# Diagonal score pieces of a gated attention kernel, cut row block by row block, with their halves on alternating PE halves and three DMA turns each

## The chip, the cores and the metric

The kernel runs on one core of a Trainium2 chip. The metric is the device time of one execution in microseconds (us); lower is better. The median of four executions of the kernel before is 1201.04 us (1200.83 to 1202.45). The engines are called by the profile's short names: PE (TensorE matmul), PEld (its weight loads), DVE (VectorE), ACT (ScalarE), POOL (GpSimd) and SP (the queue that issues most DMAs).

## The reference

```python
batch, seq, d_model = (8, 3008, 256)
d_qk = 64

def _attn_ref(u, v, z):
    scale = 1.0 / S
    scores = scale * np.matmul(z, z.transpose(0, 2, 1))
    attn = np.maximum(scores, 0.0) ** 2
    out = np.matmul(attn, v)
    return (u * out).astype(np.float32)

def _moe_ref(x, w_in, w_out):      # x: 24064 x 256, w_in: 256 x 2048
    h = x @ w_in
    g = h * np.cos(h)
    return (g @ w_out).astype(np.float32)
```

The scores come from z on both sides, so the matrix of scores of a batch is symmetric: the block of rows k and columns j is the transpose of the block of rows j and columns k. The change lives on this.

## The kernel before

**Pieces.** A batch's 3008 x 3008 scores are cut into row blocks k of 128 rows (24, the last of 64) and column groups J of 512 columns (6, the last of 448). Four row blocks make a row group I, and a piece (b, J, I) is the 512 x 512 part of batch b in column group J and row group I, held in one of 18 buffers A as relu(score) squared, in fp16. Only pieces with I >= J are computed, in two groups each, h = 0 (row blocks 4I and 4I+1) and h = 1 (4I+2 and 4I+3). The pieces above the diagonal are made by turning those below with a DMA that transposes blocks of 128 x 128. (For the first three column groups of batch 0 more is computed directly, and nothing on the diagonal is cut.)

**A score group** (`emit_score`, L182 to L224). Two matmuls at L191 write two banks of an accumulator E, one for each of the two row blocks t = 0, 1. The contraction has 64 rows. zT holds z transposed twice, on partitions 0 to 63 and again on 64 to 127, so the two matmuls can take the two halves of the PE array: t = 0 half 0, t = 1 half 1. ACT then takes the relu of both banks to r (L204), and DVE squares r into the piece's buffer (L209, or L212 on the diagonal). Once a piece is whole, it is entered in a list of pieces to be turned.

**Pieces on the diagonal** (I = J, 45 of them are cut). In its group h = 0 only the first 256 columns are computed (`W = 2 * P`), in h = 1 all. What is missing, rows 0 to 255 of columns 256 to 511, is turned from the lower left of the same piece.

**Turns** (`emit_turns`, L226 to L246). In order of the slot that needs them, SP issues one turn of 16 blocks for a piece off the diagonal (L244, into a fresh buffer) and two turns of 2 blocks for one on it (L238): for rr = 2 and 3, the row block rr's first two blocks into column block rr of rows 0 and 1.

**Value matmuls** (`emit_value`, from L257). For slot s = (b, J), `phase_a` contracts the pieces of column group J with v, in two passes over 24 row blocks, again with 64 rows at a time: t = 0 on half 0, t = 1 on half 1, always in this turn, each into a bank of its own. Between these pairs, `phase_a` puts the score groups of later slots (some three slots ahead) at even distances, each followed by `emit_turns` of one more turn. `phase_a` thus consists of half-array matmuls alone.

**Expert layers.** `phase_b` follows each `phase_a`: with the full array, h = x w_in (L403), the cosine on ACT (L411), the product on DVE (L414), and g w_out (L465 or L507). Half-array and full-array work take turns 46 times in a run.

**Order.** The program is written out by hand (`manual_schedule`): each engine runs its instructions in the order in which the code emits them, and waits for others by semaphores. SP's queue holds the turns of scores (L238, L244), of u (L160) and of z (L133), and the stores of the output (L525 to L529, L560). POOL's queue holds the loads of u, v and z (L118 to L146) and the additions on GpSimd. The landing of each of SP's DMAs is told by one of eight semaphores in turn, so an instruction that needs several DMAs waits for several semaphores.

Of the kernel before, what the change touches and what calls it, by code (L numbers as in the profile page):

```python
# [14 lines left out]
def kernel(  # L15
# [16 lines left out]
    P = 128  # L32
    H = P // 2
    CW = 512
# [12 lines left out]
    def width(J):  # L47
        return CW if J < NC - 1 else WL
# [38 lines left out]
    def new_piece(key):  # L87
        pieces[key] = free_pieces.pop(0)
        return piece_bufs[pieces[key]]

    def piece(key):
        return piece_bufs[pieces[key]]
# [10 lines left out]
    def take_e():  # L103
        i = e_order.pop(0)
        e_order.append(i)
        return i
# [75 lines left out]
    def emit_score(on_dve=False, later=None):  # L182
        b, J, I, h = groups[done_groups[0]]
        done_groups[0] += 1
        cut = I == J and not (b == 0 and J < 3)
        W = 2 * P if cut and h == 0 else width(J)
        zT = zTs[b]
        e = E[take_e()]
        for t in range(2):
            k = 4 * I + 2 * h + t  # L190
            nc.tensor.matmul(  # L191
                e[:, t, 0:W],
                zT[t * H:(t + 1) * H, k * P:(k + 1) * P],
                zT[t * H:(t + 1) * H, J * CW:J * CW + W],
                start=True,
                stop=True,
            )
        key = (b, J, I)
        a = new_piece(key) if h == 0 else piece(key)
        r = rpool.tile([P, 2, CW], FP16, name="r")  # L200
        if on_dve:
            nc.vector.tensor_scalar(r[:, :, 0:W], e[:, :, 0:W], 0.0, None, ALU.max)
        else:
            nc.scalar.activation(r[:, :, 0:W], e[:, :, 0:W], AF.Relu)  # L204
        def square():
            if I > J:
                a4 = a.rearrange("p (k t j) -> p t k j", k=4, j=P)[:, 2 * h:2 * h + 2, :, :]
                r4 = r.rearrange("p t (k j) -> p t k j", j=P)
                nc.vector.tensor_tensor(a4, r4, r4, ALU.mult)  # L209
            else:  # L210
                a4 = a.rearrange("p (k w) -> p k w", w=CW)[:, 2 * h:2 * h + 2, 0:W]
                nc.vector.tensor_tensor(a4, r[:, :, 0:W], r[:, :, 0:W], ALU.mult)  # L212

        if later is None:
            square()
        else:
            later.append(square)
        if h == 0:
            return
        if cut or (I > J and (b, J, I) not in direct):  # L220
            turns.append(((b, I), key))
            turns.sort(key=lambda t: t[0])
            turn_slots[key] = pieces[key]
            pending[pieces[key]] = "held"  # L224

    def emit_turns(due, more=0):  # L226
        while turns and (turns[0][0] <= due or more > 0):
            if turns[0][0] > due:
                more -= 1
            (b, c), key = turns.pop(0)  # L230
            b, J, I = key
            i = turn_slots[key]
            a = piece_bufs[i]
            if I == J:
                a4 = a.rearrange("p (k w) -> p k w", w=CW)
                for rr in range(2, 4):
                    rows = P if J * 4 + rr < NB - 1 else H
                    nc.sync.dma_start_transpose(  # L238
                        a4[:, 0:2, rr * P:rr * P + rows],
                        a[0:rows, rr * CW:rr * CW + 2 * P],  # L240
                    )
            else:
                d = new_piece((b, I, J))
                nc.sync.dma_start_transpose(d.rearrange("p (n j) -> p n j", j=P), a)  # L244
            if pending.pop(i) == "dropped":
                free_pieces.append(i)  # L246
# [58 lines left out]
    def phase_a(s):  # L305
        b, J = s // NC, s % NC
        emit_turns((b, J))
        n = next_scores(s)
        at = {}
# [7 lines left out]
        for i, (dh, k) in enumerate(steps):  # L317
            if dh == 2:
                emit_value(b, J, k, 0, 0, M[0], False, True)
                emit_value(b, J, k, 1, 1, acc1[1], True, False)  # L320
                gate(s, 0, M[0], M[1])
            else:
                acc = M if dh == 0 else acc1
                last = k == NB - 2
                for t in range(2):
                    emit_value(
                        b, J, k, t, dh, acc[t],
                        k == 0 and not (dh == 1 and t == 1),
                        last and not (dh == 0 and t == 0),
                    )  # L330
                if dh == 1 and (k % 4 == 3 or last):
                    drop_piece((b, J, k // 4))
            for _ in range(at.get(i, 0)):
                emit_score()
                emit_turns(divmod(s + 1, NC), 1)
            if i in mix_at and mixed(s - 2):
                mix_late(s - 2, *mix_at[i])
# [9 lines left out]
    def phase_a_first(s, n, extra={}):  # L347
# [16 lines left out]
        for i, (dh, k) in enumerate(steps):  # L364
            if i in extra:
                extra[i]()
            if dh == 2:
                emit_value(b, J, last, 0, 0, acc[0][0], False, True)
                emit_value(b, J, last, 1, 1, acc[1][1], False, True)
            else:  # L370
                for t in range(2):
                    emit_value(
                        b, J, k, t, dh, acc[dh][t], k == 0, k == last - 1 and t != dh
                    )
            if dh > 0 and (k % 4 == 3):
                drop_piece((b, J, k // 4))
                if s > 0:
                    emit_turns((0, 0), 1)
                    if k < 4:
                        turn_u(s)  # L380
                    elif k < 8:
                        for d in range(2):
                            gate_mul(s - 1, d, late_sums.pop(0))
            for _ in range(at.get(i, 0)):
                emit_score(on_dve=done_groups[0] in on_dve)
# [262 lines left out]
    turn_on_pe(1)  # L648
    copy_turned(1)
    emit_score(later=squares)  # L650
    emit_score(later=squares)
    turn_on_pe(2)
# [46 lines left out]
    for s in range(3, NSLOT + 1):  # L699
        b, J = s // NC, s % NC  # L700
# [52 lines left out]
```

## Time and profile before

| what | value |
|---|---|
| median of four executions | 1201.04 us |
| the profiled execution, its own time | 1201.03 us |
| its span, from the first instruction to the last | 1199.2 us |
| PE clock granted | full throughout |
| L191, 64 x 256 columns, matmuls | 90, busy 12.5 us |
| L191, 64 x 512 columns, matmuls | 578, busy 111.5 us |
| L258, value matmuls | 4512 |
| L204 relu of 128 x 512 (cut groups) | 45, 601 ns each |
| L212 square of 128 x 512 (cut groups) | 45, 418 ns each |
| turns of pieces (L238 and L244) | 90 and 117 |
| share of 16 DMA engines, SP's queue and POOL's | 52.5% and 28.5% |

A row of a group shows the engine, the line, what is written and read, the shape, the count, the time in which at least one of them ran ("busy") and the mean of one. A matmul's duration in such a row includes its latency, and matmuls overlap; what a matmul costs is better read from the distance of starts. In the chain of waits each row is a start in us, the time that the step holds the chain, and what ran.

### The profile page before, as it was taken

The numbers are of one execution on the slowest core, as the hardware profiler recorded it, in microseconds if no ns is written. First come the engines' busy times: TensorE is split into PE (matmuls) and PEld (weight loads), VectorE is DVE, ScalarE is ACT, GpSimd is POOL, SyncE is SP. The second block draws the span as 40 slices with busy tenths as digits, with TensorE's granted clock in tenths as the row PEclk, the third lists the DMA queues.
The fourth block names the chain that finished last, engine by engine and source line by source line (L and its number), as shares of the span: only waits on it lengthen the run. The fifth ranks groups of instructions, "written<-read, shape, count | busy, mean of one in ns | idle before, by whom it ended". The sixth has DMA issues, their size and how long they took to land.

```text
span 1199.2 us, 28321 instructions
## 1 busy us (share of the span) xinstructions
PE 1188.9 (99%) x11695; PEld 703.9 (59%) x11695; DVE 989.5 (83%) x1248; ACT 795.7 (66%) x923; POOL 642.3 (54%) x657
## 2 busy tenths in 40 slices
PE   9999999999999999999999999999999999999998
PEld 4455655665556655665556655665556555666566
DVE  6858888888988887788988889788888888878775
ACT  7957666666766666666766676666766667666444
POOL 3155735567555571665746656166565765525440
PEclk9999999999999999999999999999999999999999
DMA  9998898759996599946999469983798837974301
GB/s 158 179 158 142 133 148 114 122 103 130 133 124 120 105 135 158 130 78 119 140 144 136 79 111 149 164 114 76 114 160 151 117 71 117 165 118 89 62 19 54
DMA packets 467410, 145.13 MB, mean 121 GB/s; under 512 B 391760, under 2 KB 467024, under 8 KB 467280
## 3 DMA queue, kind: packets, MB, share of 16 engines
q1 hardware_dynamic: 368304, 110.11, 52.5%
q0 software_dynamic: 97440, 32.78, 28.5%
q8 instruction: 91, 1.49, 0.5%
q10 hardware_dynamic: 1536, 0.43, 0.2%
q14 instruction: 39, 0.32, 0.1%
HBM read 66.32 MB, written 24.64 MB: 76 GB/s over the span
## 4 chain that ended last, share of the span: by engine, by line
PE 96%; ACT 1%; DVE 1%; issue 1%; DVEq 0%; ACTq 0%
PE E L403 27%; PE M L465 21%; PE M L258 20%; PE E L258 19%; PE E L191 5%; PE M L507 4%; ACT r L204 1%; DVE g L414 0%; PE E L636 0%; DVE A L209 0%; DVE sm L270 0%; DVE A L212 0%; PE E L507 0%; DVE x L286 0%; PE M L660 0%
## 5 line engine op out<-in xcount | busy, mean ns | idle before, releaser
L411 ACT ACTIVATE c<-E 128x1024 f16<-128x1024 f32 (+1 forms) x384 | 385.7, 1006 | 224.1 <-PE E L403 223.2
L414 DVE SCALAR_TENSOR_TENSOR g<-E,c 128x1024 f16<-128x1024 f32 (+1 forms) x384 | 459.0, 1197 | 77.5 <-ACT c L411 77.0
L204 ACT ACTIVATE r<-E 128x512 f16<-128x512 f32 (+1 forms) x342 | 327.8, 966 | 115.1 <-PE E L191 110.1
L258 PEld LDWEIGHTS <-v 64*128 64x128 f16 x4512 | 225.7, 94 | 251.9 <-issue 18.4
L403 PE MATMUL E<-x,w_in 128*128 128x512 f16 (+1 forms) x1408 | 354.5, 375 | 2.7 <-DVE sm L270 2.0
L258 PE MATMUL M<-A,v 64*128 64x512 f16 (+1 forms) x2256 | 283.1, 372 | 0.3 <-DVE sm L270 0.3
L427 POOL TENSOR_TENSOR s<-g 128x512 f16<-128x512 f16 x160 | 187.1, 1169 | 176.1 <-DVE g L414 134.2
L258 PE MATMUL E<-A,v 64*128 64x512 f16 (+1 forms) x2256 | 278.1, 372 | 0.0
L428 POOL TENSOR_TENSOR g<-g 128x512 f16<-128x512 f16 x160 | 198.2, 1238 | 12.6
L403 PEld LDWEIGHTS <-w_in 128*128 128x128 f16 x1536 | 134.6, 98 | 112.4 <-issue 22.7
L209 DVE TENSOR_TENSOR A<-r 128x1024 f16<-128x1024 f16 x240 | 172.5, 730 | 21.6 <-ACT r L204 20.9
L286 POOL TENSOR_TENSOR x<-sm,uT 128x512 f16<-128x512 f32 (+1 forms) x43 | 48.6, 1130 | 244.8 <-DVE sm L270 244.5
L465 PEld LDWEIGHTS <-g 128*128 128x128 f16 x2560 | 156.4, 98 | 36.1
L465 PEld LDWEIGHTS <-s 128*128 128x128 f16 x1920 | 117.3, 98 | 27.0
L191 PE MATMUL E<-zT 64*128 64x512 f16 (+2 forms) x684 | 126.8, 363 | 1.9 <-DVE zT L631 1.1
L433 DVE TENSOR_TENSOR s<-s,g 128x1024 f16<-128x1024 f16 x80 | 90.9, 1136 | 2.1 <-POOL s L427 2.1
L212 DVE TENSOR_TENSOR A<-r 128x512 f16<-128x512 f16 (+1 forms) x102 | 76.9, 755 | 14.8 <-ACT r L204 14.3
L465 PE MATMUL M<-w_mix,s 128*128 128x128 f16 x1280 | 84.6, 219 | 0.0
L465 PE MATMUL M<-w_mix,g 128*128 128x128 f16 x1280 | 84.6, 219 | 0.0
L465 PE MATMUL M<-w_out,g 128*128 128x128 f16 x1280 | 84.6, 219 | 0.0
L191 PEld LDWEIGHTS <-zT 64*128 64x128 f16 x684 | 35.6, 94 | 41.7 <-issue 4.1
L507 PE MATMUL M<-w_out,g 128*128 128x256 f16 x432 | 55.8, 273 | 0.4 <-DVE sm L270 0.4
(55 smaller groups left out, 685.6 us busy)
## 6 DMA issues: line engine op xcount, KB each, us to landing
out_dram<-o SPq DMA_DIRECT2D x87, 256.0 KB, 2.2
v<-in_v_dram POOLq DMA_DIRECT2D x40, 256.0 KB, 8.7
u<-in_u_dram POOLq DMA_DIRECT2D x40, 256.0 KB, 4.8
A<-A SPq DMA_TRANSPOSE x207, 5.4
z<-in_z_dram POOLq DMA_DIRECT2D x14, 192.0 KB, 10.6
z<-in_z_dram POOLq DMA_DIRECT2D x14, 176.0 KB, 5.9
v<-in_v_dram POOLq DMA_DIRECT2D x8, 192.0 KB, 12.3
u<-in_u_dram POOLq DMA_DIRECT2D x8, 192.0 KB, 4.0
```

Of the source, the lines that this page charges most:

```text
L191: nc.tensor.matmul(e[:, t, 0:W], zT[t * H:(t + 1) * H, k * P:(k + 1) * P], zT[t * H:(t + 1) * H, J * CW:J * CW + W], start=True, stop=True,)
L204: nc.scalar.activation(r[:, :, 0:W], e[:, :, 0:W], AF.Relu)
L209: nc.vector.tensor_tensor(a4, r4, r4, ALU.mult)
L258: nc.tensor.matmul(bank[:, 0:width(J)], vs[b, k // 4][t * H:(t + 1) * H, k % 4, dh * P:(dh + 1) * P], value_rhs(b, J, k, t), start=start, ...
L403: nc.tensor.matmul(e[:, f, 0:W], w_in16[:, k, ft * P:(ft + 1) * P], x[:, k, 0:W], start=(k == 0), stop=(k == 1),)
L411: nc.scalar.activation(c[:, :, 0:W], e[:, :, 0:W], AF.Sin, bias=half_pi, scale=inv_s2)
L414: return lambda: nc.vector.scalar_tensor_tensor(gs[m][:, 2 * i:2 * i + 2, 0:W], e[:, :, 0:W], 1.0, c[:, :, 0:W], ALU.mult, ALU.mult)
L427: nc.gpsimd.tensor_tensor(s1[:, f, :], g[:, f, T:], g[:, lower, T:], ALU.add)
L428: nc.gpsimd.tensor_tensor(g[:, f, T:], g[:, f, 0:T], g[:, f, T:], ALU.subtract)
L433: nc.vector.tensor_tensor(s2[:, f, :], s1[:, f, :], g[:, f, 0:T], ALU.subtract)
L465: nc.tensor.matmul(acc[:, k * P:(k + 1) * P], left[:, ft, k * P:(k + 1) * P], right[:, ft, :], start=(ft == 0 and k == 0), stop=(ft == F - ...
L507: nc.tensor.matmul(y_bank(m, k), gs[m][:, ft, k * P:(k + 1) * P], w_out16[:, ft, :], start=(ft == 0 and (k % 2 == 0 or (final and k == 3)) ...
```

## The change

In `emit_score`, each matmul of a cut piece gets its own width, `Wt`: row block 0 has 128 columns, 1 has 256, 2 has 384, and 3 all of them (512, or 448 in the last column group). The half of the array follows t for h = 0, and is the other one for h = 1; this holds for every score group, cut or not. The relu and the square keep the width W of the whole group. In `emit_turns`, a piece on the diagonal has three turns, rr = 1, 2 and 3, of rr blocks each.

```diff
@@ emit_score
         for t in range(2):
             k = 4 * I + 2 * h + t
+            half = t if h == 0 else 1 - t
+            rows = slice(half * H, (half + 1) * H)
+            Wt = min(W, (2 * h + t + 1) * P) if cut else W
             nc.tensor.matmul(
-                e[:, t, 0:W],
-                zT[t * H:(t + 1) * H, k * P:(k + 1) * P],
-                zT[t * H:(t + 1) * H, J * CW:J * CW + W],
+                e[:, t, 0:Wt],
+                zT[rows, k * P:(k + 1) * P],
+                zT[rows, J * CW:J * CW + Wt],
                 start=True,
                 stop=True,
             )
@@ emit_turns
-                for rr in range(2, 4):
+                for rr in range(1, 4):
                     rows = P if J * 4 + rr < NB - 1 else H
                     nc.sync.dma_start_transpose(
-                        a4[:, 0:2, rr * P:rr * P + rows],
-                        a[0:rows, rr * CW:rr * CW + 2 * P],
+                        a4[:, 0:rr, rr * P:rr * P + rows],
+                        a[0:rows, rr * CW:rr * CW + rr * P],
                     )
```

## The prediction

> **What bounds the kernel now.** I read the page first (share of the span by engine, then the chain that ended last), then the chain piece by piece between 300 and 330 us, then the timeline of PE at a change from half arrays to full ones, and last the transfers.
>
> ```profile
> span 1199.2 us, 28321 instructions
> PE 1188.9 (99%) x11695; PEld 703.9 (59%) x11695; DVE 989.5 (83%) x1248; ACT 795.7 (66%) x923; POOL 642.3 (54%) x657
> PE 96%; ACT 1%; DVE 1%; issue 1%; DVEq 0%; ACTq 0%
> ```
>
> TensorE is busy all the time and is 96% of the chain. A busy PE need not be at its peak, so the next view is the chain itself, with the time that each step holds the chain:
>
> ```profile
> 321.10 1.40 PE M L258 x12
> 322.51 0.11 PE E L191 x2
> 322.62 1.08 PE M L258 x10
> 323.69 0.22 PE E L191 x2
> ```
>
> This is a score piece on the diagonal (L191): its upper half is the pair at 322.51, its lower half the pair at 323.69, with ten value matmuls (L258) between. All of these contract 64 rows, so two run at once, one on partitions 0 to 63 (half 0) and one on 64 to 127 (half 1). Ten matmuls of 512 columns take 1.08 us, that is 0.216 us for a pair; a pair of 256 columns takes 0.11 us. So the time goes by the columns, 0.42 ns each, and not by the "270" or "376" ns that a matmul's row shows, which hold its latency too. Placed by their starts in this way, the 11,695 matmuls leave next to no gap from 100 us on, but for one kind:
>
> ```profile
> 305.73 0.38 PE L191 MATMUL E<-zT 64*128 64x512 f16 x2
> 305.95 1.89 PE L258 MATMUL E<-A,v 64*128 64x512 f16 x16
> 307.77 1.04 PE L403 MATMUL E<-xodd,w_in 128*128 128x512 f16 x4
> ```
>
> Eight pairs from 305.95 end at 307.68; the full array starts at 307.77, 0.09 us later. The same 0.09 us stands at nearly every change between half and full arrays. So the end is set by TensorE's columns, and what this change is worth is the columns that really leave the longer half.
>
> **What goes.** 45 diagonal pieces are cut (3 of batch 0, 6 of each of the other seven). Upper half: the first matmul goes from 256 to 128 columns, the second stays at 256. Lower half: the first from 512 to 384, the second stays at 512 (for the 8 pieces of the last column, 448 to 384, and 448 stays). In each pair only one gets shorter. In the upper half the short one is on half 0; in the lower half the program issues the short one first, and on half 1, then the long one on half 0. If both were on half 0, half 1 would be as long as before and nothing could come of it. As it is, half 0 saves 128 columns in the upper pair and half 1 saves 128 in the lower, 54 ns each. To bank them, half 0 must run 54 ns ahead from the upper pair to the lower one. In 39 of the 45 pieces both pairs lie in the same stretch of half-array work; in 6 full-array work comes between, which waits for both halves and loses the lead.
>
> **The size, from both sides.** That a lead can last is seen in the trace: from 197.9 to 209.0 us half 1 starts its matmuls 39 to 55 ns after half 0, through 54 pairs, with neither half closing up. At best, then: 37 pieces x 54 ns + 8 x 27 ns = 2.2 us, less the 6 that lose it (0.3 us) = 1.9 us. At worst nothing: at the lower pair the order is value matmul on half 0, value matmul on half 1, short score on half 1, long score on half 0. Half 0 is free 54 ns before half 1, but the long score stands behind the short one in PE's stream. If PE starts matmuls in program order, the long one waits for the short one's start, and the 54 ns are idle on half 0. From there the long score of 512 columns ends at the very instant at which it ended before; half 1 is done 54 ns earlier, but its next value matmul stands behind that of half 0, and waits likewise. The gain is 0 on every piece. No row decides it: in the profiled program the halves alternate strictly, half 0 first, so no matmul ever stands behind one of the other half that is later.
>
> **Two rules of the Trainium skill pull apart here.** "TensorEngine Tiling (Array Packing)", section "Key Properties", says that tiles work independently and can run matmuls in parallel; taken alone it promises the 1.9 us, and the lasting lag of 39 to 55 ns agrees with it. "TensorE: Matmul & The Clock Gate", section "Part 3: Packing small matmuls", says that matmuls start and end in program order, a strict FIFO in which only weight loads are pulled ahead. By that the sum is 0. The trace agrees as far as it goes (pairs start in step, 3 ns within a pair as a rule), but has no place that could contradict it. The two fit together: independent once started, started in order. I take 0 here.
>
> **The turned order has a price of its own, and more pieces pay it than gain.** The new line for the half looks at h alone, so each of the 171 lower pairs changes order, the 45 cut ones and 126 whole ones. Within a pair the second matmul starts about 3 ns after the first. The first score takes half 1 at +3 ns, the second half 0 at +6, so half 0 resumes some 6.6 ns late: 171 x 6.6 ns = 1.1 us, if matmuls start in order; if not, half 0 never waits and it is 0. Weight loads should be no obstacle: each half's next load starts 2 ns after the matmul before it on that half has started, under it, and in the new order too every load has the length of a matmul to run in. But two matmuls in succession on one half stand nowhere in the trace, so the bounds of a turn are 0 and the 0.09 us of the nearest row, the change of array shape. I take the 6.6 ns, by the rows of pairs, since the shape (64 x 128) stays.
>
> **The engines behind.** ScalarE's relu (L204) and VectorE's square (L212) still take the full width, 256 or the column's, reading leftovers in the corner that the third turn then writes over; 45 relus of 601 ns and 45 squares of 418 ns stay. No gain, no cost.
>
> **The turns.** Per piece two turned transfers of 2 blocks become three of 1, 2 and 3: 45 more issues on the SP queue and 90 more blocks of 128 x 128.
>
> ```profile
> L238 SPq DMA_TRANSPOSE A<-A x90: 1167/1202/2432, 59.3 to 1117.0; - x90
> DMA to landing us min/median/max: 2.3/4.7/9.1
> ```
>
> One issue holds SP 1.2 us whatever its 2 blocks, and an 8-block one of u 1.6, so the sum is 45 x 1.2 = 54 us on a queue whose issues now add up to 675 of 1199 us; 1.2 to 1.6 us later for what is queued behind. What is queued: turns of other pieces (landing 15.8 us or more before the first matmul that reads them), of u (9 us or more after slot 0, mostly 27 to 41), of z (11.8 us or more), and stores of the output (over 10 us before their buffer is written again; the last few, which have less, come after all turns). The diagonal turns themselves land 14 to 42 us before their use, except those of the first cut piece: issued at 59.3 and 60.9 us, the second lands 9.1 us later, 5.1 us before its value matmul at 75.1. The third one, issued at about 62.5, should land near 72: 3 us left. So the queue costs 0 while TensorE covers it. Load of the DMA engines: a block is 128 packets of 256 B of 26 ns over 16 engines, 0.21 us; 90 blocks are 19 us, 1.6% of the span. The tightest transfers are the loads of v at a batch's change (window 280 to 300 us, DMA share 1.39): 3.0 us of slack, of which one piece takes 0.4. Were this cover gone, each late microsecond would be one of the span.
>
> Weight loads that wait for two transfers or more rise from 8 to 46; the first of the two then stands as an instruction of its own on PE, 51 ns in the 7 places at batch starts that have it now, without a gap in the matmuls there, since PE's sequencer is over a microsecond ahead. Bounds 0 and 38 x 51 ns = 1.9 us; I take 0, by those rows.
>
> **Sum.** The profiled execution took 1201.03 us (span 1199.2 and 1.8 around it), the median is 1201.04: 1201.03 - 0 + 1.1 = **1202.1 us**.
>
> **Rivals.**
> - *The halves do slip past each other* (each takes its matmul when it is free): 1201.03 - 1.9 = 1199.1 us. For it: the persistent lag. Against it: order of issue. Chance 0.25. It is 0.16%, so even the full gain lies inside the 0.2% (2.4 us) that a measurement of this kernel can tell from no change.
> - *Turning the order of the halves drains the array*: at the full 0.09 us for each of 171 lower pairs 15.4 us, 1216.4 us. It decides from 14 ns a turn (2.4 us). For it: nothing in the trace has run in this order, and it is paid 171 times against 45 gains. Against it: the shape stays, and weights are loaded under a matmul of the same half already. Chance 0.20.
> - *A transfer comes late*: the third turn at 75 us, or v at the seven changes of batch. It needs more than 3 us of extra delay, then perhaps 0.5 us each, 3.5 us in all: 1204.5 us. Chance 0.05.
>
> **Numbers.** The main case 0.48, the rivals 0.25, 0.20 and 0.05, and 0.02 for something else. Faster by over 0.2% needs more than the slip can give: 0.05, for the slip with luck. Slower by over 0.2%: the drain, late transfers, or the main case with the waits on PE added: 0.27. Within: 0.68. The range takes in the first two cases, the 1.9 us of waits on PE on top of the main one, and turns of up to some 23 ns: 1198.8 to 1205.0 us.
>
> **What would show it.** Right: in the chain the upper pair of a cut piece holds 0.05 us and then half 1 trails by 54 ns; at the lower pair both scores start within 4 ns of each other, the first as late as half 1 is free, and from the upper pair's start to the end of the stretch nothing is shorter than before. The slip is shown if the long score starts before the short one, or the stretch is 54 ns shorter per piece. The drain is shown by a gap of up to 0.09 us at every lower pair, cut or not; late transfers by waits of value matmuls for A or v. I am wrong outright if the time leaves 1198.6 to 1203.4, the bounds of no change.

## The result and the profile after

The changed kernel takes 1199.67 us (median of 41 runs, 1199.30 to 1201.45), the one before 1201.03 us (61 runs). The ratio is 0.999, with a 95% interval of 0.9985 to 0.9994. The profiled execution took 1199.69 us, 1.34 us less than before's, with a span of 1197.9 us. In the kernel before and in most of those below, a part of the executions takes 1.1 to 1.5 us longer, and in the four profiles that fell among them (e6, e7, e9, e10) TensorE's clock is halved for 3.4 us near 90 us (the last section shows it), so a median depends on how many of them it holds. Below, TensorE's part is therefore read from the starts of its matmuls in the trace, after that place.

The page of the changed kernel, the lines that answer to those shown of before:

```profile
span 1197.9 us, 28487 instructions
PE 1187.1 (99%) x11695; PEld 734.6 (61%) x11695; DVE 989.6 (83%) x1248; ACT 795.6 (66%) x923; POOL 642.8 (54%) x657
PE 96%; ACT 1%; DVE 1%; issue 1%; DVEq 0%; ACTq 0%
```

TensorE still sets the end. The chain of the changed kernel, at the piece that was shown of before (start, time that the step holds the chain, what ran):

```profile
320.67 1.40 PE M L261 x12
322.08 0.11 PE E L194 x2
322.19 1.08 PE M L261 x10
323.26 0.16 PE E L194 x2
323.43 0.86 PE M L261 x8
```

The upper pair still holds the chain for 0.11 us, the length of its long matmul, but the lower pair holds it for 0.16 us where it held 0.22. That is 54 ns, the 128 columns. So the columns saved on half 0 in the upper pair and those saved on half 1 in the lower pair were both banked: the halves slipped past each other. The timeline of the changed kernel around another piece shows the slip itself (start, time until the last of the group ends, group):

```profile
102.86 0.27 PE L194 MATMUL E<-zT 64*128 64x128 f16 x2
102.92 1.30 PE L261 MATMUL M<-A,v 64*128 64x512 f16 x10
104.00 0.38 PE L194 MATMUL E<-zT 64*128 64x512 f16 x2
104.21 0.81 PE L261 MATMUL M<-A,v 64*128 64x512 f16 x6
```

The first value matmul starts 0.06 us after the upper pair, when the 128-column one is done. A group carries the shape of its first member by time: the upper pair is headed by the 128-column matmul, the lower one by the one of 512 columns. In the program the 384-column matmul stands first. Each start in the trace:

| start, us | matmul | place in the program |
|---|---|---|
| 103.995 | score, 512 columns, half 0 | second of the lower pair |
| 104.052 | score, 384 columns, half 1 | first of the lower pair |
| 104.211 | value, 512 columns, half 0 | next pair, first |
| 104.214 | value, 512 columns, half 1 | next pair, second |

The halves of the two value matmuls follow from the scores before them: each starts when the score on its half is through (512 columns 216 ns, 384 columns 162 ns). The long score did not wait for the short one that stands ahead of it. Both halves are level again at 104.21, and the stretch from the upper pair to there is 53 ns shorter than before.

Summed over the run: TensorE's last matmul ends 1.84 us earlier than before, in steps of 52 to 55 ns in each stretch of half-array work with one whole cut piece, about 80 in those with one of the last column group beside it, and 2 to 4 ns where a lower pair lies alone. (The first cut piece, in the stretch from 41.9 us on, gained nothing; TensorE waits for other engines there.) From the last matmul to the last instruction, though, it is 4.35 us where it was 3.84. So 1.84 - 0.51 = 1.33 us of the span remain.

### The profile page after: what moved, and what is told of

The parts are those of the page before. It is cut to its first block, busy times and chain, and to the rows that moved or that the text cites. A ratio compares the mean times of both kernels' runs of the same rounds, so it can differ in the third digit from the quotient of the medians.

```text
span 1197.9 us, 28487 instructions
## 1 busy us (share of the span) xinstructions
PE 1187.1 (99%) x11695; PEld 734.6 (61%) x11695; DVE 989.6 (83%) x1248; ACT 795.6 (66%) x923; POOL 642.8 (54%) x657
## 3 DMA queue, kind: packets, MB, share of 16 engines
q1 hardware_dynamic: 380752, 112.93, 54.5%
## 4 chain that ended last, share of the span: by engine, by line
PE 96%; ACT 1%; DVE 1%; issue 1%; DVEq 0%; ACTq 0%
PE E L406 27%; PE M L468 21%; PE M L261 20%; PE E L261 19%; PE E L194 5%; PE M L510 4%; ACT r L207 1%; DVE g L417 0%; PE E L639 0%; DVE A L212 0%; DVE sm L273 0%; DVE A L215 0%; PE E L510 0%; DVE x L289 0%; PE M L663 0%
## 5 line engine op out<-in xcount | busy, mean ns | idle before, releaser
L261 PEld LDWEIGHTS <-v 64*128 64x128 f16 x4512 | 252.6, 94 | 223.2 <-issue 19.6
L194 PE MATMUL E<-zT 64*128 64x512 f16 (+4 forms) x684 | 128.9, 357 | 1.9 <-DVE zT L634 1.1
L194 PEld LDWEIGHTS <-zT 64*128 64x128 f16 x684 | 39.6, 94 | 37.6 <-issue 3.7
```

Of the source, the lines that this page charges most:

```text
L194: nc.tensor.matmul(e[:, t, 0:Wt], zT[rows, k * P:(k + 1) * P], zT[rows, J * CW:J * CW + Wt], start=True, stop=True,)
L261: nc.tensor.matmul(bank[:, 0:width(J)], vs[b, k // 4][t * H:(t + 1) * H, k % 4, dh * P:(dh + 1) * P], value_rhs(b, J, k, t), start=start, ...
```

## Experiments

Starts are compared with those of the kernel before, from the half-array stretch at 101.6 us to the last one; the changed kernel gains 1.76 us there (the other 0.08 us lie earlier). "Tail" is the time from the end of the last matmul to the last instruction.

| kernel | starts from 101.6 us on | tail, us | its own time when profiled, us | median, us |
|---|---|---|---|---|
| before | 0 | 3.84 | 1201.03 | 1201.03 |
| the change | -1.76 | 4.35 | 1199.69 | 1199.67 |
| e1 halves turned, nothing cut | -0.01 | 3.85 | 1200.61 | 1200.98 |
| e2 cut, halves not turned | -0.01 | 4.34 | 1201.57 | 1201.34 |
| e3 third turn alone | 0.00 | 4.35 | 1201.54 | 1201.60 |
| e4 change with two turns | -1.76 | 3.83 | 1199.24 | 1200.21 |
| e5 halves exchanged | -1.76 | 4.35 | 1199.71 | 1199.73 |
| e6 long score first | -1.76 | 4.34 | 1201.07 | 1199.75 |
| e7 lead of up to three matmuls | -10.79 | 4.35 | 1192.04 | 1192.15 |
| e8 six stores more | -1.76 | 3.81 | 1199.02 | 1199.14 |
| e9 eight stores more | -1.76 | 4.03 | 1200.58 | 1199.41 |
| e10 lead of up to seven | -32.9 | 4.36 | 1169.86 | 1169.08 |

**e1: the turned order by itself.** Theory 1 (order): starts keep the program's order. Theory 2 (slip): a half takes its next matmul when it is free.

```diff
-            Wt = min(W, (2 * h + t + 1) * P) if cut else W
+            Wt = W
-                for rr in range(1, 4):
+                for rr in range(2, 4):
```

(and the two turns of before, 2 blocks each)

> Only the halves are turned in the 171 lower pairs; widths and two turns per piece are those of before. If matmuls of the two halves start in program order, each turned pair costs 6.6 ns: 1.1 us more than before in the starts of TensorE's matmuls, 1202.1 us. If each half takes its next matmul as soon as that half is free, 0: 1201.0 us. If a turn drains the array, up to 15.4 us more.

The chain of this kernel at the piece near 322 us, whose lower pair is turned:

```profile
322.12 0.11 PE E L194 x2
322.23 1.08 PE M L261 x10
323.31 0.22 PE E L194 x2
```

The turned pair holds the chain as long as the straight one did before, 0.22 us. The 171 turned pairs cost nothing: the sum of the starts differs by 0.01 us, and the ratio to before is 1.0001 (0.9991 to 1.0011). The 1.1 us of my sum is not there, nor any drain.

**e2: shorter columns on one half alone.**

```diff
-            half = t if h == 0 else 1 - t
+            half = t
```

> Widths cut and three turns, as in the change, but each row block on the half it had before, so both short matmuls fall on half 0. By either theory half 1 is as long as before: TensorE's last matmul starts at the same time as before (0.0 us), against 1.84 us earlier with the change. The end carries the third turns' price alone: 1201.5 us if the longer wait at the end (0.5 us in the profile after) comes with them, 1201.0 if not.

The chain of this kernel at the piece of 102.86 us above:

```profile
103.19 0.11 PE E L194 x2
103.30 1.08 PE M L261 x10
104.38 0.22 PE E L194 x2
```

The same step before, and with the change:

```profile
104.29 0.22 PE E L191 x2
104.21 0.16 PE E L194 x2
```

(The chain sets its steps some 0.2 us later than the starts in the timeline.) The lower pair holds 0.22 us, as before. The same columns are left out as with the change, yet no time is gained, since half 1 is as long as it was. So the gain lies in the balance, not in the columns.

**e5: the halves exchanged.** Here half 1 gets the lead, and value matmuls would have to overtake.

```diff
-            half = t if h == 0 else 1 - t
+            half = 1 - t if h == 0 else t
```

> The halves of the change exchanged: the upper pair turned, the lower not. Now half 1 gets the lead, so a value matmul of half 1 would have to start before the one of half 0 that stands ahead of it in the program, pair after pair. If a half takes its matmul when free: 1.84 us earlier as with the change. If only a score pair could do that (a property of that place), or if starts keep the order: 0 to 1.1 us later.

The timeline of this kernel:

```profile
102.87 0.27 PE L194 MATMUL E<-zT 64*128 64x256 f16 x2
102.93 1.29 PE L261 MATMUL M<-A,v 64*128 64x512 f16 x10
104.01 0.38 PE L194 MATMUL E<-zT 64*128 64x512 f16 x2
104.22 0.59 PE L261 MATMUL M<-A,v 64*128 64x512 f16 x4
```

The 256-column matmul on half 0 now starts first, and 0.06 us later a value matmul runs, on the half that had 128 columns: half 1, whose value matmul stands second in its pair. The lower pair starts at 104.01 and the next at 104.22, as with the change. The gain is the same 1.76 us. It isn't a property of the score pairs.

**e6: the order that needs no overtaking.**

```diff
-        for t in range(2):
+        for t in (range(2) if h == 0 else (1, 0)):
```

> The change with the two matmuls of a lower pair exchanged in the program, the long one on half 0 first, the order that would give the gain even if starts kept the program order. If halves are independent: the same as the change, TensorE's last matmul 1.84 us earlier than before, same time as the change. If starts kept program order, this kernel would be ahead of the change by 1.8 us or more.

The gain is the same, 1.76 us, so there was nothing left for this order to give.

**e7: how far ahead?** The pieces on the diagonal have full pairs on their usual halves here.

```diff
+        whole = I > J and not (b == 0 and J < 3)    # n_whole starts at 0
+        if whole:
+            n_whole[0] += 1
+            side = (n_whole[0] - 1) // 4 % 2
-            half = t if h == 0 else 1 - t
-            Wt = min(W, (2 * h + t + 1) * P) if cut else W
+            half = (t if side == 0 else 1 - t) if whole else t
+            Wt = P if whole and t == 0 else W
```

> How far may a half run ahead? In every score group off the diagonal (batch 0's first three columns aside) one matmul keeps only 128 of its 512 columns (the other 384 are left out, leftovers take their place), and the short one lies on half 0 for four groups, then on half 1 for four, so that one half can get up to 640 ns ahead, three matmuls. If a half never waits for the other: 10.7 us less than before in TensorE's starts. If it may pass just one waiting matmul of the other half: 7.0 us less; if two: 10.5. In program order: 0.7 us more.

10.8 us less, the value for halves that don't wait, or pass at least two. Single stretches say more: in those at 150.4, 444.3, 738.1 and 1031.9 us a limit of two waiting matmuls would give 432 ns (2 x 216) and no limit 480 (three matmuls shorter by 160 each); measured were 484, 479, 482 and 481. So at least three can be passed.

**e10: the limit.** Ten value matmuls in a row are short on half 0, then ten on half 1.

```diff
+        W = width(J)
+        if b * NC + J > 3 and dh == 0 and 2 <= k < 22 and t == (0 if k < 12 else 1):
+            W = P
```

(The product is written, and the piece read, with this W.)

> How deep is the lead at most? From slot 4 on, in the first pass over v, ten value matmuls in a row on half 0 keep 128 of their columns (the rest is left out), then ten on half 1, so half 0 could get 1.6 us ahead, over seven full matmuls, and the half behind catches up. If a half never waits for the other: TensorE's matmuls 70 us less than before in all. If it may pass at most one waiting matmul of the other half: 15 us less; two 25, three 34, four 42, five 50, six 58. The runs so far exclude one and two.

32.9 us, next to the 34 of a limit of three, and far from 25 and 42. In the stretches one by one it is the same: at 101.6, 126.8 and 150.4 us the gain was 790, 602 and 844 ns, against 807, 621 and 863 for three, and 592 to 648 or 810 to 1023 for two or four. Some 18 ns a stretch are missing. The starts show the limit itself, and part of this rest: at 814.79 us half 0 is free for its next short value matmul, but four earlier ones of half 1 have not started; the first of them starts at 814.878 us, and the short one 8 ns later. So a start that the limit held back comes 8 ns after its release (8 or 9 ns in nearly all of some 300 such places); the rest of the 18 ns stays open. Part of the chain of this kernel:

```profile
297.36 0.19 PE E L194
297.55 0.22 PE E L264 x2
297.77 0.03 PE E L194
297.79 1.08 PE E L264 x10
```

Single score matmuls stand in the chain, 0.4 us apart, where a pair stood before: the partners of a pair start at quite different times.

This also answers a question that the slip raises. Only the second score matmul of a pair, by its place in the program, signals that the pair is done, and the relu on ACT waits for that signal. What if the second is far ahead of the first? Three rows of this kernel's timeline, a lower pair whose 384-column matmul stands first in the program:

```profile
814.46 0.39 PE L194 MATMUL E<-zT 64*128 64x512 f16 x1
815.09 0.32 PE L194 MATMUL E<-zT 64*128 64x384 f16 x1
815.46 1.02 ACT L207 ACTIVATE r<-E 128x1024 f16<-128x1024 f32 x1 [0.55 <-PE E L194]
```

The 512-column matmul, which signals, starts 0.64 us before its partner and passes three waiting ones of the other half (two value matmuls and the partner). Yet ACT, idle for 0.55 us, starts 0.04 us after the end of the partner, and 0.62 us after that of the signalling one (the profile models these ends, but the difference is far beyond that). In the 173 pairs of e7 and e10 with a lead of over 0.25 us this way round, no relu starts less than 44 ns after the end of the first matmul. So the starts leave the program's order, but the signal comes as if they did not.

**e3 and e4: what the third turn costs.** e3 has the three turns alone; e4 has all but the third turns.

```diff
# e3
-            half = t if h == 0 else 1 - t
-            Wt = min(W, (2 * h + t + 1) * P) if cut else W
+            half = t
+            Wt = W
```

> The third turn alone: widths and halves as before, three turns of 1, 2 and 3 blocks per diagonal piece. TensorE's matmuls start as before (within 0.05 us up to the last one). If the third turns cause the longer wait after the last matmul, the end is 0.5 us later than before, 1201.5 us; if that wait has another cause, 1201.0 us.

```diff
# e4: the turns of before
-                for rr in range(1, 4):
+                for rr in range(2, 4):
-                        a4[:, 0:rr, rr * P:rr * P + rows],
-                        a[0:rows, rr * CW:rr * CW + rr * P],
+                        a4[:, 0:2, rr * P:rr * P + rows],
+                        a[0:rows, rr * CW:rr * CW + 2 * P],
```

> The matmuls and halves of the change with the two turns per piece of before (left out: filling block (0,1) and block (2,3) of each diagonal piece, so these hold leftovers). TensorE's last matmul 1.84 us earlier than before; after it the wait of before. 1199.2 us, 0.5 us ahead of the change, if the wait at the end comes with the number of transfers; 1199.7 us if it does not.

Clear in both: with the third turns the tail is 4.35 us, without 3.83, whatever the matmuls do, and the starts are those of before in e3 and those of the change in e4. By the profiled executions e3 took 1201.54 us and e4 1199.24. So the change is worth 1.84 us on TensorE and pays 0.51 us at the end of the program.

**e8 and e9: where the 0.51 us lie.** At the end SP waits for the eight landing semaphores in a fixed order. In the trace each wait takes 0.06 us once its DMA has landed. With the change (and in e3) the last landing, 2.74 us after the last matmul, is the second in that order and six waits follow it; before, it was the fifth and three followed. That is 3 x 0.06 = 0.19 us. Besides, 0.33 us pass between two of the waits after it, where 0.03 is usual: 0.30 us more. Both add up to the 0.5 us. e8 moves the last landing to the last place with six more DMAs; e9 adds eight, one round of the eight semaphores, which leaves it where it is and only lengthens SP's program.

```diff
+        elif J == 0 and half == 0 and 1 <= b <= 6:      # e9: without the condition on b
+            for j in range(2):
+                nc.sync.dma_start(out[t0 + j * P:t0 + (j + 1) * P, :], o[:, j, :])
```

> The change with six of the output's stores split in two, so that SP issues six more DMAs and the last transfer of all falls on the last of the eight landing semaphores in the order in which SP waits for them at the end. If the waits behind the last landing cost 0.06 us each, six fewer of them take off 0.38 us against the change, and the 0.3 us pause between two of those waits goes too if it hangs on them: 1199.0 to 1199.3 us. If the end does not hang on it: 1199.7 us.

> Eight more DMAs on SP than the change (eight stores split in two): with eight landing semaphores in turn, the last transfer falls on the same one as with the change, only SP's program is longer. TensorE's last matmul 1.84 us earlier than before. If the place in the order of waits sets the end, six waits stand behind the last landing as with the change, and the end is 4.3 us after the last matmul (3.8 with e8); if the 0.3 us pause among them depends on where SP's program lies, it moves: 4.0 us, or 4.3 if it does not.

e9's tail is 4.03 us: six waits still follow the last landing, but the pause is gone. So 0.19 us go with the place among the semaphores, and the pause does not: it went when SP's program got eight issues longer. One thing stands beside it in every trace. Where the pause is seen (the change, e2, e3, e5, e6, e7, e10), a packet of 8 KB on queue q14, of the kind "instruction", starts some 3.75 us after the last matmul, 0.6 us behind the pause; in e8 and e9 it starts 1.0 and 1.6 us ahead of the last matmul's end, and in the kernel before, e1 and e4 there is none in the last 20 us. So the pause seems to hang on where SP's program comes to a new block of instructions; that the block causes it is not shown. In e8 the tail is 3.81 us, and TensorE's gain is whole. Its page:

```profile
span 1197.2 us, 28487 instructions
```

e8 took 1199.02 us when profiled, its median is 1199.14 us, the ratio to before 0.998 (0.9971 to 0.9988). It is ahead of both kernels; against the change, by the 0.53 us of the tail. In e8 no pause is seen after the last landing; whether one lies hidden ahead of it stays open.

## Why the prediction was wrong

- **The step that failed** is the choice at the two rules: "If PE starts matmuls in program order, the long one waits for the short one's start", and "I take 0 here". The trace of before had no place to decide it, as the prediction said, and I let the rule in "TensorE: Matmul & The Clock Gate", section "Part 3: Packing small matmuls", decide against the one in "TensorEngine Tiling (Array Packing)", section "Key Properties". The runs decide for the second: starts don't keep the program's order when the halves have work of different length. My reading "independent once started, started in order" is refuted by the starts at 103.995 and 104.052 us and by e5, e7 and e10. What keeps the order here is the signal that a pair is done (e10).
- **The price of the turned order**, "171 x 6.6 ns = 1.1 us", fell with it. I had written that it is 0 if matmuls don't start in order; e1 measured 0.01 us. With the right branch the sum would have been the rival's 1199.1 us.
- **The rival's size** was right: 1.9 us worked out from columns, 1.84 measured; the loss in the 6 pieces whose pairs lie in different stretches shows as gains of 2 to 4 ns where a lower pair is alone.
- **The third turns** cost more than I gave them, at a place that I hadn't looked at. "So the queue costs 0 while TensorE covers it" holds up to the last matmul (e3: 0.00 us), but at the end nothing covers SP, and 0.51 us were lost. This is why the result is not at 1199.1 us but at 1199.7.
- **What held**: SP's issues rose by 61 us (54 said). The third turn of the first cut piece landed at 71.7 us, 3.4 us before its use (near 72, 3 us). SP's queue took 54.5% of the 16 DMA engines where it took 52.5%, 2.0 points (1.6 said). The 45 instructions more on PE that wait for a semaphore (38 said) made no gap: the stretches gain their 52 to 55 ns whole. Neither a drain nor a late transfer came.
- **The range** says nothing for the mechanism. The time fell by 0.11% where the sum had it rise by 0.09%. It lies between 1198.8 and 1205.0 us, and within the 0.2% that I called no change, but the sum of 1202.1 and the rival's 1199.1 us both lie there, so that was no test of the reasoning.

## What to carry to other kernels

When two row halves of the PE array work on matmuls of different length, add up the columns of each half over the whole stretch between two full-array pieces of work: the longer sum is the time, and not the sum of each pair's longer one, so long as one half doesn't have to pass more than three waiting matmuls of the other. Shortening one matmul of a pair gains only if its partner half is shortened elsewhere in the same stretch (e2 against the change). And a DMA that is hidden in mid-kernel may still cost at the end, where the queue's last waits lie open: look at what follows the last landing.

## What the runs showed of the hardware

- A half-array matmul passes waiting ones of the other half that stand ahead of it in the program, three at most here: 480 ns of lead were gained in full (e7), and where 1.6 us were on offer, the gain was that of three matmuls (e10). Each of these matmuls has its own weight load, so a limit that counts loads as well would look the same.
- The signal of a matmul that ran ahead waits for the one before it in the program: with a lead of 0.64 us the relu started 0.04 us after the end of the later one (e10).
- Turning the order of the halves, so that two matmuls in succession lie on one half, costs nothing (171 times, 0.01 us).
- At about 87 us VectorE is late and TensorE stands still for 2 us, in all kernels. In four of the twelve profiles the clock is halved soon after it, for 3.4 us. First the row of e6 with the wait, then its windows (TensorE's clock is the third figure from the end, before DMA share and GB/s):

```profile
89.02 1.02 PE L406 MATMUL E<-x,w_in 128*128 128x512 f16 x4 [1.98 <-DVE sm L273]
84.00:88.00 4.00, 3.04 (x22) 2.05 (x21) 1.80 (x4) 2.18 (x3) 3.06 (x4) 1.00 0.89 100
88.00:92.00 4.00, 2.98 (x14) 1.74 (x14) 4.00 (x5) 1.02 (x1) 4.00 (x7) 0.74 1.40 152
92.00:96.00 4.00, 4.00 (x25) 2.52 (x24) 1.59 (x2) 1.79 (x2) 0.51 (x2) 0.83 1.47 170
```

The granted clock was 0.74 and 0.83 in the windows after the gap, and 1.00 in the same windows of the changed kernel; what is missing, 0.26 and 0.17 of 4 us, makes 3.4 us at half the clock. Why the clock falls in some executions and not in others, after the same gap, is not shown. It costs as much as the whole change gains, so a kernel without that gap would be worth a try.
